# A transformer layer on one core: a third attention job in the lead, its exps held in K and V areas

## The chip, the core and the metric

The kernel runs on one core of a Trainium2 chip. The core has a matrix engine (TensorE, PE in the profile), a vector engine (VectorE, DVE), an engine for functions such as exp (ScalarE, ACT), a general one (GpSimd, POOL) and one that issues transfers (SyncE, SP). They run side by side and wait for one another by semaphores. TensorE writes its results to PSUM, eight banks of 128 x 512 fp32; everything else lies in SBUF. The metric is the device time of one execution in microseconds (us), less is better.

## What is computed

One transformer layer over 2048 tokens with 1024 features, in bf16:

```python
h  = x + softmax_attention(layernorm(x) @ wqkv) @ wo      # 32 heads of 32
h2 = h + gelu(layernorm(h) @ w1 + b1) @ w2 + b2           # 3584 hidden features
```

Softmax is over all 2048 keys, with no mask, so 32 x 2048 x 2048 exps are needed.

## The kernel before

**Units and jobs.** The tokens are cut into eight units of 256 (UNITS); heads are taken four at a time, g = 0 to 7, four heads filling the 128 partitions. A job (k, g) is the attention of unit k for head group g: eight rounds of 256 keys. One round is: `Att.qk` (L925 to L953) issues eight matmuls (QK, line L941 in the profile) into four PSUM banks, and two exps over 128 x 1024 each (L952) into a buffer PT. `Job.pv` (L989) then multiplies the exps with V (L996, PV) into a fifth bank. The softmax's denominators are sums over the keys, made by a matmul with ones (`den`, L1027, line L1036). To make it cheaper VectorE first adds the two 256-column halves of a round's exps (first-level sum, L1013), and for units below QA pairs of such sums (second-level sum, L1019); a round that is "direct" skips VectorE and goes through the ones-matmuls whole. `DIRECT` says how many of the last rounds of a job are direct (1; 3 in the very last job), `QUAD` which units have second-level sums (QA = 8: all). `finish` divides and writes the result to OT. Six PSUM banks take scores in three pairs of two; two banks (6, 7) are left for everything else, PV's result among it.

**Buffers.** There are NR = 9 PT buffers. For the lead eight more, PX 0 to 7, are laid into areas of K and V that are not written yet (L531 to L538). x tiles arrive in xrb, eight slots that overlap the later PS (VectorE's sums) and OT.

**The lead.** Before attention can run freely, x has to be normalized and projected. Sixteen tiles of 128 tokens are loaded (`x_tile`, L786), normalized on VectorE (`layer_norm`, L717: statistics L715, aggregate L724, small casts L728 to L738, a power on GpSimd L736, normalize L741), transposed on TensorE (L763) and copied from PSUM to xnT, by ScalarE (L770) for the tiles in LEAD_ACT (ten of sixteen), by VectorE (L772) for the others. For each half chunk hc (two tiles, 256 tokens) `proj_half` (L898) makes K of head group 0, and Q for hc 0 and 1; `proj_v1` (L885) makes V of group 0. As soon as a piece of K is there, the rounds of jobs (0, 0) and (1, 0) that it allows are issued: their exps go to PT and PX and are held, because the first PV waits for all projections of the lead (`pv_last`). After that come the two jobs' PVs. Before the first transposes N_WARM = 50 matmuls on zeros run (L1262).

**The rest.** ORDER (L1279) lists the jobs that run beside the projections of the further head groups (`rest_of_projections`, L1329: Q of units 0 and 1, all of K and V): (2, 0), (3, 0), then for g = 1 to 7 units 0 and 1. The weights for them are loaded after the last x tile (`rest_w`). Then unit by unit: the output projection `wo` (L1099), a second layernorm `ln2`, Q of later units (`late_q`, L844), `ffn1` and `ffn2`, beside the attention of the units that follow. K, V, xnT and the weights share their areas with the feed-forward part, so that starts only when the projections are finished. The last unit's feed-forward part has no attention beside it.

**What sets the order.** Each instruction group is a Task with an estimated duration and a priority. `Graph.schedule` (L110) runs a list scheduler over these estimates when the kernel is built, and each engine's program is emitted in the order it found; at run time an engine takes its instructions strictly in that order. VectorE, ScalarE, GpSimd and SP pick the ready task of the lowest `prio`; TensorE follows `pick_pe` (L1417): scores first, then PV by PV_BEGIN and PV_MUST, then background work by `turn`. Tables of shifts (GROUP_SHIFT, PRIO_SHIFT), keyed by the numbers of groups and tasks, move single tasks.

Of the kernel before, what the change touches and what calls it, by code (L numbers as in the profile page):

```python
# [13 lines left out]
BF = dt.bfloat16  # L14
F32 = dt.float32
# [46 lines left out]
class Graph:  # L62
# [47 lines left out]
    def schedule(self, pick_pe, pool, switch=(0.11, 0.106, 0.1), dma_rate=340.0, dma_first=1.6, dma_tail=1.0, dma_issue=0.42,  # L110
# [32 lines left out]
        while n < total:  # L143
# [5 lines left out]
            for e in self.ENGS:  # L149
                while free[e] <= now + 1e-9:  # L150
# [12 lines left out]
                    else:  # L163
                        t = min(rd, key=lambda x: (x.prio, num[x]))
                        if up and t.prio > 0:

                            for (rt, _, u) in up[:6]:
                                if u.prio < t.prio and rt < now + 0.6 * t.occ:
                                    t = None
                                    break  # L170
# [159 lines left out]
    def emit(self, e, obj):  # L330
# [10 lines left out]
PV_BEGIN = "6887668783765478677666734877585674766834855865775635885656674536"  # L341
PV_MUST = "2563656375427345237632753323452322425663763553734473555222232667"
GROUP_SHIFT = (
        "0:-229 1:131 2:136 6:-161 8:-202 9:133 11:142 14:17 15:-143 16:-115 17:-197 18:-131 20:-226 22:18 "
        "26:-18 28:-97 32:-17 33:177 34:-29 39:56 40:-11 42:55 44:53 45:81 46:22 48:243 50:-360 51:-22 "
        "55:-161 56:-142 57:-12 61:-20 66:-4 68:-18 69:18 72:-25 73:-7 76:-9 78:-61 83:-51 84:5 88:-36 "
        "89:-80 91:-37 92:-13 93:-18 94:6 95:125 98:-125 100:-193 101:-23 104:132 105:226 106:91 111:401 "
        "112:505 113:205 117:-165 118:182 120:-316 121:-313 122:-8 123:-383 124:-11 127:54 131:-14 133:-43 "
        "134:-32 135:-435 136:-33 138:-391 141:-7 145:-13 150:102 160:-184 163:3 165:232 166:-25 167:-29 "
        "169:-162 174:-10 175:592 176:-1 177:626 178:17 179:99 180:-167 182:-21 183:116 184:-46 185:11 "  # L350
        "186:24 187:-51 197:-74 198:-215 199:13 200:81 201:-20 202:4 207:-50 208:-4 209:172 211:-27 214:118 "
        "215:-55 216:-45 219:385 230:-13 231:14 232:-7 233:72 234:-5 235:78 236:-65 238:135 239:-593 240:29 "
        "241:-111 244:-185 245:112 247:-121 248:22 250:39 251:104 252:15 261:50 264:-4 268:220 270:-530 "
        "271:5 272:-920 273:1 274:-176 276:-54 277:91 279:24 281:31 293:171 294:13 295:123 296:-33 298:-6 "
        "299:111 300:113 301:2 305:321 308:34 310:17 311:10 313:52 315:-85 326:3 328:-4 329:-160 330:-11 "
# [94 lines left out]
def build_kernel(nc, A_x, A_wqkv, A_wo, B_w1, B_b1, B_w2, B_b2, out):  # L450
# [807 lines left out]
    for tt in range(4, 8):  # L1258
        x_tile(tt, -5)
# [274 lines left out]
```

## Time and profile before

| | |
|---|---|
| runs shown | 5466.11, 1078.71, 1082.22 us; median 1082.22 |
| profiled execution, its own time | 1079.89 us |
| its span | 1078.0 us |
| first exp / end of the last exp | 17.69 / 1017.7 us |
| VectorE's sums | first level x446 (439 + 7 on PX), second level x191 |
| granted TensorE clock | 1.00 |

The profile is of one execution. "Busy" is the share of the span in which an engine's instructions run; a matmul's end is modelled. A group of instructions is named by its line in the kernel, its engine and its operands (out<-in). The number after "idle before" is the time its engine stood still just before it, and the name after the arrow what ended that. The chain is the work that ended last, followed back from the end.

### The profile page before, as it was taken

The page shows a single profiled execution, that of the slowest core. Times are in us where ns is not written, and L with a number is a line of the kernel's source. Part 1 is how long each engine was busy: PE and PEld are TensorE (multiplying, and loading weights), DVE is VectorE, ACT ScalarE, POOL GpSimd, SP SyncE. Part 2 cuts the span into 40 slices and gives each one's busy share as a digit, 9 for nine tenths or more (in the row PEclk, how much of TensorE's full clock was granted, in tenths as well). Part 3 has the DMA queues.
Part 4 walks back from the last instruction along what each step waited for, and adds up shares of the span by engine and source line. Part 5 has one row for each costly group of instructions (what it writes and reads, how often), then busy time and mean ns, then how long its engine had stood idle before and what let it go on. Part 6 is the DMA issues. An engine that isn't in the chain of part 4 may idle for free.

```text
span 1078.0 us, 38343 instructions
## 1 busy us (share of the span) xinstructions
PE 1037.0 (96%) x17162; PEld 586.8 (54%) x17162; DVE 887.6 (82%) x1737; ACT 1016.2 (94%) x1121; POOL 18.8 (2%) x35
## 2 busy tenths in 40 slices
PE   7889999999999999999999999999999999999998
PEld 5546555554446645654466457456645644564483
DVE  8888677777789997998789979988997997997711
ACT  4999999999999999999999999999999999999850
POOL 2000000000000000000000000000000000000000
DMA  7910010005656575754686667558575755987640
GB/s 196 256 60 3 13 49 2 2 2 175 205 153 204 149 224 167 220 164 132 222 259 183 189 197 203 163 173 260 150 222 184 210 150 162 290 258 236 192 153 20
DMA packets 265492, 173.93 MB, mean 161 GB/s; under 512 B 26864, under 2 KB 259952, under 8 KB 264944
## 3 DMA queue, kind: packets, MB, share of 16 engines
q1 hardware_dynamic: 265328, 171.48, 53.1%
q8 instruction: 135, 2.21, 0.8%
q14 instruction: 29, 0.24, 0.1%
HBM read 161.09 MB, written 10.35 MB: 159 GB/s over the span
## 4 chain that ended last, share of the span: by engine, by line
ACT 85%; PE 10%; DVE 3%; DMA 2%; issue 0%; SPq 0%; DVEq 0%
ACT PT L952 79%; PE ps L672 5%; ACT tg L1215 4%; PE ps L669 3%; ACT PX L952 1%; PE ps L941 1%; DMA a_w1r<-in_B_w_dram 1%; DVE st L715 1%; ACT xnT L770 1%; DMA xrb<-in_A_x_dram 0%; PE ps L996 0%; DVE PS L1013 0%; DMA a_w1r<-in_A_wo_dram 0%; DVE xb L741 0%; DVE gT L1192 0%
## 5 line engine op out<-in xcount | busy, mean ns | idle before, releaser
L952 ACT ACTIVATE PT<-ps 128x1024 bf16<-128x1024 f32 x1008 | 937.4, 1148 | 5.4 <-PE ps L941 5.2
L1013 DVE TENSOR_TENSOR PS<-PT 128x1024 bf16<-128x1024 bf16 x439 | 297.4, 684 | 78.1 <-ACT PT L952 52.1
L941 PE MATMUL ps<-QT,KT 32*128 32x256 bf16 x4096 | 203.6, 273 | 13.6 <-ACT PT L952 9.9
L996 PE MATMUL ps<-PT,V 128*32 128x256 bf16 x4032 | 160.5, 273 | 2.9 <-DVE gT L1192 1.1
L941 PEld LDWEIGHTS ps<-QT,KT 32*128 32x128 bf16 x4096 | 60.8, 92 | 170.0 <-ACT PT L952 157.8
L669 PE MATMUL ps<-hnT,a_w1r 128*128 128x256 bf16 x1197 | 148.1, 273 | 1.8 <-DMA a_w1r<-in_B_w_dram 0.7
L1019 DVE TENSOR_TENSOR PS<-PS 128x1024 bf16<-128x1024 bf16 x191 | 130.8, 685 | 3.4
L669 PE MATMUL ps<-a_w2r,gT 128*128 128x512 bf16 x510 | 125.7, 380 | 3.7 <-DVE hnT L772 1.2
L669 PEld LDWEIGHTS ps<-hnT,a_w1r 128*128 128x128 bf16 x1197 | 109.2, 98 | 35.3 <-issue 20.3
L996 PEld LDWEIGHTS ps<-PT,V 128*32 128x32 bf16 x4032 | 100.9, 96 | 37.5 <-issue 6.3
L666 PE MATMUL ps<-a_w2r,gT 128*32 128x512 bf16 x1096 | 80.2, 382 | 0.4 <-DVE gT L1192 0.2
L669 PEld LDWEIGHTS ps<-a_w2r,gT 128*128 128x128 bf16 x510 | 43.8, 98 | 61.9 <-issue 15.0
L1036 PE MATMUL ps<-PS,ones 128*32 128x256 bf16 x1020 | 70.5, 274 | 0.8 <-DVE PS L1013 0.5
L1192 DVE TENSOR_TENSOR gT<-ps,b1f 128x512 bf16<-128x512 f32 x98 | 66.7, 684 | 4.8 <-PE ps L669 2.4
L666 PE MATMUL ps<-hnT,a_w1r 128*32 128x256 bf16 x1484 | 54.5, 274 | 1.7 <-DMA a_w1r<-in_B_w_dram 0.6
L1215 ACT ACTIVATE tg<-tg 128x1024 bf16<-128x1024 bf16 x49 | 55.6, 1148 | 0.0
L669 PE MATMUL ps<-xnT,Wall 128*128 128x512 bf16 (+1 forms) x241 | 51.9, 345 | 2.5 <-ACT xnT L770 1.6
L669 PE MATMUL ps<-Wall,xnT 128*128 128x256 bf16 x345 | 45.6, 274 | 1.4 <-DVE KT L819 0.8
L666 PEld LDWEIGHTS ps<-hnT,a_w1r 128*32 128x32 bf16 x1484 | 36.3, 96 | 13.4 <-issue 11.2
L666 PE MATMUL ps<-xnT,Wall 128*32 128x512 bf16 x540 | 39.1, 381 | 0.6 <-DVE KT L819 0.6
L1244 DVE SCALAR_TENSOR_TENSOR b_ost<-ps,hch 128x512 bf16<-128x512 f32 x4 | 2.8, 692 | 44.7 <-PE ps L672 44.7
L669 PEld LDWEIGHTS ps<-Wall,xnT 128*128 128x128 bf16 x345 | 31.2, 98 | 12.7 <-issue 5.1
(101 smaller groups left out, 998.0 us busy)
## 6 DMA issues: line engine op xcount, KB each, us to landing
a_w2r<-in_B_w_dram SPq DMA_DIRECT2D x105, 512.0 KB, 4.8
a_w1r<-in_B_w_dram SPq DMA_DIRECT2D x98, 512.0 KB, 4.8
a_w1r<-in_A_wo_dram SPq DMA_DIRECT2D x32, 512.0 KB, 4.5
b_w1r<-in_B_w_dram SPq DMA_DIRECT2D x14, 512.0 KB, 5.0
a_w1r<-in_A_wqkv_dram SPq DMA_DIRECT2D x11, 512.0 KB, 4.0
xrb<-in_A_x_dram SPq DMA_DIRECT2D x16, 256.0 KB, 4.1
Wall<-in_A_wqkv_dram SPq DMA_DIRECT2D x16, 256.0 KB, 4.6
hch<-in_A_x_dram SPq DMA_DIRECT2D x16, 256.0 KB, 4.4
```

Source lines behind the costliest of these rows:

```text
L666: fns.append(lambda p, j=j: p.matmul(psum[32 * j:32 * j + 32, bi(bank), c0:c1], lhsT[:, 32 * j:32 * j + 32], rhs, start=start, stop=stop, ...
L669: t.whole = lambda p: p.matmul(psum[:, bi(bank), c0:c1], lhsT, rhs, start=start, stop=stop, skip_group_check=True)
L672: t = pe(lambda p: p.matmul(psum[:, bi(bank), c0:c1], lhsT, rhs, start=start, stop=stop), occ, reads=reads, writes=[bb(bank)], mode="full" ...
L715: return dve(lambda v: v.bn_stats(st_l[:, i, 6 * c:6 * c + 6], src), 0.6, reads=[B_src], writes=[B_stl[i][c]], prio=prio)
L941: return p.matmul(psum[:, 2 * us[h // 2] + h % 2, n * i:n * i + n], KT[32 * h:32 * h + 32, g, k0:k0 + P], QT[32 * h:32 * h + 32, qs, 0:n], ...
L952: act(lambda a, u=u, k=k: a.activation(pt(s)[:, k, :, :], psum[:, 2 * u:2 * u + 2, :], ACT.Exp, bias=0.0, scale=SCALE), 1024, reads=[B_ps[ ...
L996: fns.append(lambda p, i=i, h=h: p.matmul(psum[32 * h:32 * h + 32, bi(bank), 0:nq], V[:, g, nk * r + i, 32 * h:32 * h + 32], pt(s)[:, h // ...
L1013: dve(lambda v: v.tensor_tensor(PS[:, n, :, :], pairs[:, :, 0:256], pairs[:, :, 256:512], ALU.add), c_dve(1024, 2), reads=[B_PT[2 * s], B_ ...
L1019: dve(lambda v: v.tensor_tensor(PS[:, n, :, :], PS[:, n, :, :], PS[:, m, :, :], ALU.add), c_dve(1024, 2), reads=[B_PS[n], B_PS[m]], writes ...
L1036: fns.append(lambda p, h=h, rhs=rhs, i=i: p.matmul(psum[32 * h:32 * h + 32, bi(bank), nq:2 * nq], ones32[:, :], rhs, start=False, stop=las ...
L1192: drop(dve(lambda v: v.tensor_tensor(gT[:, fc:fc + 2, cs], psum[:, bi(bank), 0:2 * n].rearrange("p (f c) -> p f c", f=2), b1f[:, fc:fc + 2 ...
L1215: act(lambda a: a.activation(t, t, ACT.Tanh, bias=0.0, scale=math.sqrt(2.0 / math.pi)), c, reads=B_t, writes=B_t, prio=-1)
```

## The change

**Lead.** Job (2, 0) joins (0, 0) and (1, 0). PX grows from eight to fourteen: K and V areas of g = 1 to 4, K of 5 to 7, V of 5, and two in slots 4 to 7 of xrb; so x tiles 12 to 15 now go to slots 0 to 3 and are loaded ahead of 8 to 11, which go to slots 4 to 7. Tile 0 is loaded in two halves, tile 1 ahead of the Q weight, tile 2 ahead of the K weight. Tiles 0 to 3 are normalized one by one in strict order. Q is made for hc 0, 1, 2 and 3 by halves (units 2 and 3 came in one projection of 512 before); for hc 0 and for all of K the matmuls are 128 columns wide. LEAD_ACT keeps tiles 0 to 3; the other twelve copies are VectorE's. ScalarE copies K and Q of hc 0 and 1 and V of the first two tiles. Warm-up matmuls: 34 instead of 50, into bank 3 instead of 4. Round 7 of job (2, 0) follows job (0, 0)'s PVs. While t < 16 us in its estimates the scheduler may hold VectorE for a more urgent task that is about to be ready.

**Sums.** The three lead jobs are direct in all rounds (no VectorE sums). Second-level sums stay for units 0 to 5 (QA = 6).

**Order of jobs.** After the lead: (3, 0); g = 1 with units 0 to 3; g = 2 to 4 with units 0 and 1; then unit 0 with g = 5 to 7, then unit 1 with g = 5 to 7. So Q of units 2 and 3 for g = 1 is made with the projections, and OT has two more slots. Mode-change costs, the transfers' sizes in the estimates and all four tables differ as well.

```diff
+LEAD_HOLD = 16.0
+LEAD_45 = 2
+LATE = 3
+DLEAD = 3
+NEX = 2
+V_ACT = 1
...
-                        if up and t.prio > 0:
+                        if up and (t.prio > 0 or e == E.DVE and now < LEAD_HOLD):
                             for (rt, _, u) in up[:6]:
-                                if u.prio < t.prio and rt < now + 0.6 * t.occ:
+                                if u.prio < t.prio and rt < now + (0.6 if t.prio > 0 else 0.4) * t.occ:
...
-    for k in range(8):
-        lo = att_lo + 2 * S * (k + 2 if k < 6 else G + k - 2)
+    px_at = [att_lo + 2 * S * a for g in range(1, 5) for a in (g, G + g)] + [att_lo + 2 * S * a for a in (5, 6, 7, G + 5)]
+    px_at += [top.cur + 2 * D * 4, top.cur + 2 * D * 6]
+    for k, lo in enumerate(px_at):
...
-    N_WARM = 50
-    LEAD_ACT = [0, 1, 2, 3, 4, 6, 8, 10, 12, 14]
+    N_WARM = 34
+    LEAD_ACT = [0, 1, 2, 3]
...
-        for dc in range(DC):
-            mm(bank, Wall[:, wp(blk), dc, 0:P], xnT[:, tc, dc, 256 * h:256 * h + 256], dc == 0, dc == DC - 1,
-               [B_W[wp(blk)][0]] + B_xnTt[tc][2 * h:2 * h + 2], True, cols=(0, 256))
+        n = P if hc == 0 or which == 1 else 256
+        for c in range(0, 256, n):
+            for dc in range(DC):
+                mm(bank, Wall[:, wp(blk), dc, 0:P], xnT[:, tc, dc, 256 * h + c:256 * h + c + n], dc == 0, dc == DC - 1,
+                   [B_W[wp(blk)][0]] + B_xnTt[tc][2 * h + c // P:2 * h + (c + n) // P], n > P, cols=(c, c + n))
...
-    QA = 8
+    QA = 6
...
-        return 0 if qb < DA else 1
+        return 16 if g == 0 and qb < DLEAD else 1
...
-    x_tile(0, -6)
+    x_tile(0, -6, 2)
+    x_tile(1, -6)
     load_w(WQ, -5, 0, P)
-    x_tile(1, -5)
+    x_tile(2, -5)
     load_w(WK, -5, 0, P)
-    x_tile(2, -5)
-    x_tile(3, -5)
-    for tt in range(4, 8):
+    for tt in range(3, 8):
         x_tile(tt, -5)
...
-        if hc == 0:
-            ln_tiles(tts[:1], -6, "dve", True)
-            ln_tiles(tts[1:], -5, "dve", True)
+        if hc < 2:
+            for tt in tts:
+                ln_tiles([tt], tt - 12, "dve", True)
...
-    ORDER = [(2, 0), (3, 0)] + [(k, g) for g in range(1, G) for k in range(2)]
+    ORDER = [(3, 0)] + [(k, g) for g in range(1, G - LATE) for k in (range(4) if g < NEX else range(2))]
+    ORDER += [(k, g) for k in range(2) for g in range(G - LATE, G)]
...
-        for k, r in {0: [(0, 0)], 1: [(0, 1), (1, 0), (1, 1)]}.get(hc, [(0, hc), (1, hc)]):
-            lead.append((k, r, att.qk((k, 0), r, NR + r if k else None)))
-    if ORDER[0] == (2, 0):
-        proj(0, 0, 1, slot(), "dve", direct=True)
-        made.append(0)
+        for k, r in {0: [(0, 0)], 1: [(0, 1), (1, 0), (1, 1)], 2: [(0, 2), (1, 2), (2, 0), (2, 1), (2, 2)]}.get(hc, [(0, hc), (1, hc), (2, hc)]):
+            if (k, r) != (2, 7):
+                lead[k, r] = att.qk((k, 0), r, None if k == 0 else NR + r if k == 1 else NR + 8 + r if r < 6 else NR - 1)
+    att.rounds = NR
+    proj_half(0, 3, slot(), "dve")
+    made.append(0)
     for hc in range(8):
-        proj_v1(2 * hc, 0, 2, slot(), "dve")
+        proj_v1(2 * hc, 0, 2, slot(), "act" if hc < V_ACT else "dve")
...
-    for k in range(2):
+    for k in range(3):
         job = Job(k, 0, slot(2))
-        for k_, r, s in lead:
-            if k_ == k:
-                job.pv(r, s)
+        for r in range(job.nr):
+            job.pv(r, lead[k, r])
+        if k == 0:
+            lead[2, 7] = att.qk((2, 0), 7)
```

## Prediction, on record before the changed kernel was seen

> **What bounds the kernel now.** I read the page first, then busy time by stage, then ScalarE's instructions in the first 30 us, then who TensorE waits for.
>
> ```profile
> span 1078.0 us, 38343 instructions
> ...
> PE 1037.0 (96%) x17162; PEld 586.8 (54%) x17162; DVE 887.6 (82%) x1737; ACT 1016.2 (94%) x1121; POOL 18.8 (2%) x35
> ...
> ACT  4999999999999999999999999999999999999850
> ...
> ACT 85%; PE 10%; DVE 3%; DMA 2%; issue 0%; SPq 0%; DVEq 0%
> ...
> L952 ACT ACTIVATE PT<-ps 128x1024 bf16<-128x1024 f32 x1008 | 937.4, 1148 | 5.4 <-PE ps L941 5.2
> ```
>
> ScalarE carries the end: 1024 exps (1008 here, 16 more into PX), full in all slices but the first and the last two. So time is won where ScalarE is not doing exps: the lead, or the tail after the last exp. The mean of 1148 ns overlaps the next instruction; a new exp starts every 0.905 us (in the fence below, four from 26.75 to the next start at 30.36), and that is its price here.
>
> ```profile
> core 0: us, PE busy (x) PEld busy (x) DVE busy (x) ACT busy (x) POOL busy (x), PEclk, DMA share, GB/s
> ...
> 51.00:61.00 10.00, 9.35 (x216) 6.57 (x217) 4.99 (x10) 9.52 (x11) 0.00 (x0) 1.00 0.68 278
> 61.00:267.00 206.00, 197.91 (x3482) 109.90 (x3473) 159.82 (x285) 205.92 (x226) 0.00 (x0) 1.00 0.10 30
> 267.00:1010.00 743.00, 723.71 (x12432) 400.12 (x12420) 663.37 (x1276) 739.18 (x805) 9.95 (x14) 1.00 0.66 197
> ```
>
> From 61 to 1010 ScalarE idles under 4 us, but TensorE only 8.1 + 19.3 = 27.4 us: a close second bound.
>
> ```profile
> 10.90 1.02 ACT L770 ACTIVATE xnT<-ps 128x1024 bf16<-128x1024 bf16 x1 [8.89 <-PE ps L763]
> ...
> 17.69 1.02 ACT L952 ACTIVATE PT<-ps 128x1024 bf16<-128x1024 f32 x1
> 18.59 1.03 ACT L770 ACTIVATE xnT<-ps 128x1024 bf16<-128x1024 bf16 x1
> 19.50 1.04 ACT L952 ACTIVATE PT<-ps 128x1024 bf16<-128x1024 f32 x1
> 22.00 1.02 ACT L770 ACTIVATE xnT<-ps 128x1024 bf16<-128x1024 bf16 x1 [1.45 <-PE ps L763]
> 24.02 1.02 ACT L952 ACTIVATE PT<-ps 128x1024 bf16<-128x1024 f32 x1 [1.00 <-PE ps L941]
> 24.94 1.02 ACT L770 ACTIVATE xnT<-ps 128x1024 bf16<-128x1024 bf16 x1
> 25.84 1.03 ACT L952 ACTIVATE PT<-ps 128x1024 bf16<-128x1024 f32 x1
> 26.75 3.80 ACT L952 ACTIVATE PX<-ps 128x1024 bf16<-128x1024 f32 x4
> 30.36 2.02 ACT L952 ACTIVATE PT<-ps 128x1024 bf16<-128x1024 f32 x2
> ```
>
> The reader sees the first exp at 17.69, copies of transposes (L770) between the exps, and waits for TensorE. By 61 us only 37 exps have started, of 48 that fit into the 43 us since the first.
>
> **The change, part by part.** The sum is made against the profiled execution: 1079.89 us, 1.89 more than its span, 2.3 under the median of 1082.22; of the other two runs shown one is 1078.71, the other no measure.
>
> *First exp earlier.* In VectorE's order tile 0's mean cast (6.92) stands behind tile 1's statistics, which wait for a transfer until 6.31, and its reciprocal (9.44) behind tile 2's; so its transposes start at 10.25. Now tile 1 is sent ahead of the Q weight and the four first tiles are normalized in strict order. From the rows: data at 3.47, two statistics 1.29, aggregate 0.21, two casts and an add near 0.4, the power on GpSimd 0.56, reciprocal and normalize 0.67, with handovers 6.8. The cover then is the warm-up: 27 of its matmuls start 0.213 us apart until 8.4, the rest 0.109 apart, so 34 of them end at 2.47 + 27 x 0.213 + 7 x 0.109 = 9.0. Tile 0's transposes start near 8.7, tile 1's follow, two copies 0.9 apart end at 11.1, K and Q in 128-column halves (second halves 16 x 0.056 = 0.9) and their copies (0.38) give the first scores at 12.5 and the first exp at 13.0: 4.7 earlier. Bounds: 1.5 (only the transposes' shift) and 5.6 (warm-up not in the way). I take 4.7, the working from rows.
>
> By the Trainium skill ("TensorE: Matmul & The Clock Gate", Part 1) matmuls run at half rate until some 3.4 us of sustained activity, and again after an idle window of that length. The trace agrees with the first half (0.213, then 0.109 after about 6 us) though its granted clock reads 1.00; if the shorter warm-up left such a gap, the lead's next 3.4 us of matmuls would take up to twice as long, by an estimate from that page 1.7 us or so off this term.
>
> *Copies.* Six copies leave ScalarE (tiles 4, 6, 8, 10, 12, 14): 6 x 0.905 = 5.4 us. Against that one V copy and one more pair of K and Q copies, 3 x 0.3 = 0.9. On VectorE the six cost 0.60 each (L772), 3.6; from its lead go 21 first-level sums and 9 second-level ones (the three lead jobs send every round's exps to the ones-matmuls directly), 30 x 0.60 = 18, most of it now after 42 us. Had VectorE no such relief, the last K half would come 3.6 later.
>
> *Third job.* Each 256-token half of K frees six exps instead of four: 6 x 0.905 = 5.4 us of ScalarE, against VectorE's feed of one half: 4 statistics 2.4, small ones 0.6, two normalizes 0.9, two copies 1.2, K and V 0.66, together 5.7. Halves 1 and 2 free 6 and 10, so ScalarE carries a stock ahead of a feed that is 0.3 slower, and the 1.45 and 1.00 waits go. I let it run through from 16.5 (second half's K; 2 exps done before). At 61 us it has started 2 + (61 - 16.5 - 0.3)/0.905 = 50.8 exps instead of 37: 13.8 x 0.905 = 12.5 us ahead, in which the first two terms are contained. Bounds: 8 (half 1 is fed as late as now, at 23.6 less the 4.7, and one hiccup per half of 0.3) and 13.5. I take 12.
>
> Cover in this stage: the held exps need buffers until the first PV, which waits for all the lead's projections. PX 0 to 11 lie in K and V of g = 1 to 4, in K of 5 to 7 and V of 5, so K of g = 1 can only be written after job 1's first PV. Today the lead's last V matmuls end near 54.9; the VectorE sums at 42.5 to 48.3 that delay the last copies are gone, so I expect about 48, lead PVs to 60, K of g = 1 from about 53. It is due when (3,0), 16 exps after the 48, is through: near 73. That wait costs nothing. SP's x tiles come in another order (12 to 15 ahead of 8 to 11), 4.1 us to landing against a half's 5.7: nothing. The weights of later g queue behind the last x tile as today.
>
> *TensorE after 61.* It must finish the same background work 12 us sooner. Removed from that stretch: QK of 6.9 rounds done earlier, each 0.218 and two mode changes of 0.13, 3.3; and the third job's PVs (8 x 0.2185) and today's sums for it (0.656), 2.4. Added: units 6 and 7 without second-level sums, 47 more groups of four ones-matmuls at 0.109, 5.1. (The lead's direct sums, 21 x 0.2185 - 12 x 0.109 = 3.3, fall before 61.) Demand 12 - 3.3 - 2.4 + 5.1 = 11.4 us out of the 27.4 idle. VectorE is relieved in units 6 and 7 by 47 x 0.60 = 28 us, which empties TensorE's two free banks sooner. No row shows how much of the idle time can be filled: between nothing (11.4 given back) and all (0). The best-filled stage has 0.8% idle, the mean is 2.9%, so up to 20 us look usable; I take a third of the demand, 4 us, as given back: nearer to all filled, since even the best stage leaves about a quarter of the mean's idle time (0.8 of 2.9) and the others start from more. Moving (2,1) and (3,1) forward and units 0 and 1 of g = 5 to 7 apart leaves 16 jobs ahead of (0,7) both ways: nothing. The tail's last second-level sum (0.6) goes, but TensorE is full there: nothing.
>
> By the Trainium skill ("Perfetto Trace Analysis", Identifying the Most-Contended Engine) headroom of TensorE is judged by weight-load share, not matmul occupancy; here that share is 53%, so nothing would be given back. TensorE's lead of the chain (10%) says otherwise.
>
> Sum: 1079.9 - 12 + 4 = 1072.
>
> **Rivals.**
> *All of it is kept* (chance 0.20). TensorE's idle time is only ScalarE's pace seen from the other side (its longest listed wait is for exps to free scores' banks, 9.9 us), and faster evictions in units 6 and 7 take 3 us off ScalarE's waits: 1079.9 - 12 - 3 = 1065. Against: 460 to 660 has under 2% idle.
> *The projections become the bound* (0.15). They end today at 267, just when job (0,7) needs the last K chunk (ScalarE waits there at 268). Demand up to that point is 12 - 5.7 + 1.7 (Q of units 2, 3 of g = 1) = 8 against 8.1 idle us. With none of it fillable, 8 to 10 go back there: 1077.
> *Slower* (0.15): TensorE is the bound from the first PV on. If that PV comes no earlier than today's 54.97, all 8.4 us of new ones-matmuls land on a full TensorE, less the 3.3 of QK: 1079.9 + 5.1 = 1085. It decides at the first PV's time. For it: 96% busy; against: 10 us of TensorE idle in the lead.
> *The lead stalls outright* on a buffer or a transfer (0.03): over 1104.
>
> **How the numbers follow.** Forecast 0.47, 1072, its own range 1068 to 1076. The range 1063 to 1083 takes in the first two rivals and the lower edge of the third, leaving out under 2 in 10. Two per cent, about what a measurement of this kernel can tell from no change, is 1060.6 to 1103.9 around the median: faster 0.03 (needs the first rival and 4 us more), slower 0.04 (the last rival and a little of the third), within 0.93.
>
> **What would show it.** First exp near 13.0 and 50 exps by 61 us (under 46: the lead term failed). Four L770 copies. First PV near 48. ScalarE's idle time in 61 to 1000 no more than 4 us above today's; if it lies before 260, the second rival is right; if late, units 6 and 7's ones-matmuls. VectorE's second-level sums 135 instead of 191, busy time down some 43 us with no effect of its own. Last exp near 1010 instead of 1017.7, the tail as long as now.

## The result and the profile after

| | before | after |
|---|---|---|
| median of 20 runs each | 1082.55 us | 1076.85 us |
| ratio | | 0.995, 95% interval 0.994 to 0.996 |
| profiled execution / its span | 1079.89 / 1078.0 us | 1075.47 / 1073.6 us |
| first exp / last exp starts | 17.69 / 1016.5 us | 15.10 / 1011.9 us |
| exps started by 61 us | 37 | 46 |

The change is 5.7 us faster in the median and 4.4 in the profiled executions. One of the 20 runs before took 5466.11 us; the ratio and its interval leave it out. Four lines of the page after it (span; busy time by engine; ScalarE's tenths in 40 slices; the chain by engine):

```profile
span 1073.6 us, 40115 instructions
...
PE 1030.0 (96%) x18065; PEld 599.5 (56%) x18131; DVE 845.1 (79%) x1668; ACT 1012.0 (94%) x1118; POOL 18.7 (2%) x36
...
ACT  5999999999999999999999999999999999999850
...
ACT 76%; PE 17%; DMA 4%; DVE 2%; issue 1%; SPq 0%; POOL 0%; POOLq 0%; DVEq 0%
```

The picture is the old one: exps from the first slice to the last but two, VectorE 42.5 us less busy. What is new is TensorE's share of the chain, 17% for 10%. Where the time was won and lost is read from the start of the n-th exp:

| exp number | 0 | 2 | 64 | 128 | 192 | 256 | 512 | 768 | 1023 |
|---|---|---|---|---|---|---|---|---|---|
| before, us | 17.7 | 24.0 | 86.0 | 144.6 | 203.5 | 262.2 | 512.3 | 763.8 | 1016.5 |
| after, us | 15.1 | 19.7 | 78.1 | 136.7 | 198.3 | 256.8 | 506.5 | 757.8 | 1011.9 |
| earlier by | 2.6 | 4.4 | 7.9 | 7.9 | 5.1 | 5.3 | 5.8 | 6.0 | 4.6 |

The lead wins 7.9 us, 2.8 go back between exps 128 and 192, 0.5 by the last exp, and the tail is as long as before. (The fall from 6.0 to 4.6 at the end is no new wait: of the tanh activations of the feed-forward part, line L1230, 15 now stand between exps 512 and 768 and 20 behind them, where 17 and 18 stood, and each takes ScalarE about 0.94 us.) The lead first: ScalarE's instructions from 9 to 20 us of the changed kernel (start, duration, engine, line, operation; in brackets the idle time before and what ended it):

```profile
9.35 1.02 ACT L767 ACTIVATE xnT<-ps 128x1024 bf16<-128x1024 bf16 x1 [7.33 <-PE ps L760]
11.55 1.02 ACT L767 ACTIVATE xnT<-ps 128x1024 bf16<-128x1024 bf16 x1 [1.18 <-PE ps L760]
13.29 0.38 ACT L920 ACTIVATE QT<-ps 128x256 bf16<-128x256 f32 x1 [0.71 <-PE ps L669]
...
14.18 1.02 ACT L767 ACTIVATE xnT<-ps 128x1024 bf16<-128x1024 bf16 x1
15.10 1.93 ACT L967 ACTIVATE PT<-ps 128x1024 bf16<-128x1024 f32 x2
16.91 1.04 ACT L767 ACTIVATE xnT<-ps 128x1024 bf16<-128x1024 bf16 x1
17.81 0.41 ACT L898 ACTIVATE V<-ps 128x256 bf16<-128x256 f32 x1
18.66 0.39 ACT L920 ACTIVATE KT<-ps 128x256 bf16<-128x256 f32 x1 [0.43 <-PE ps L669]
19.66 1.02 ACT L967 ACTIVATE PT<-ps 128x1024 bf16<-128x1024 f32 x1 [0.61 <-PE ps L956]
```

The four copies L767 are there, and the first two exps come at 15.10. The third comes only at 19.66, because tile 3's copy (16.91) stands behind those two exps and the second half's K hangs on it. TensorE in the same stretch:

```profile
8.70 0.61 PE L760 MATMUL ps<-ident,xb 128*128 128x128 bf16 x8
9.15 0.60 PE L1276 MATMUL ps<-b2t,ident 128*128 128x256 bf16 x4
10.52 0.55 PE L669 MATMUL ps<-xnT,Wall 128*128 128x128 bf16 x7 [0.77 <-ACT xnT L767]
10.90 0.61 PE L760 MATMUL ps<-ident,xb 128*128 128x128 bf16 x8
```

Tile 1's transposes (10.90) stand behind seven matmuls of tile 0's projection, which wait for tile 0's copy. Then the stages:

```profile
12.00:61.00 49.00, 40.92 (x708) 29.25 (x708) 36.52 (x103) 45.86 (x54) 4.48 (x7) 1.00 0.83 223
...
61.00:267.00 206.00, 200.92 (x3816) 117.18 (x3824) 154.58 (x281) 203.64 (x223) 0.00 (x0) 1.00 0.11 34
267.00:1010.00 743.00, 719.05 (x12996) 407.18 (x13032) 632.73 (x1222) 738.60 (x804) 9.13 (x14) 1.00 0.66 196
```

The columns are, after the stretch and its length, busy PE, PEld, DVE, ACT and POOL, then clock, DMA share and GB/s. From 61 to 267 us ScalarE now idles 2.36 us, where it idled 0.08. The whole of it is four waits for scores:

```profile
141.18 44.10 ACT L967 ACTIVATE PT<-ps 128x1024 bf16<-128x1024 f32 x48 [0.50 <-PE ps L956]
185.85 3.77 ACT L967 ACTIVATE PT<-ps 128x1024 bf16<-128x1024 f32 x4 [0.57 <-PE ps L956]
190.31 5.60 ACT L967 ACTIVATE PT<-ps 128x1024 bf16<-128x1024 f32 x6 [0.69 <-PE ps L956]
196.51 71.61 ACT L967 ACTIVATE PT<-ps 128x1024 bf16<-128x1024 f32 x78 [0.60 <-PE ps L956]
```

In the program these are four rounds whose two exps stand in swapped order on ScalarE. The next QK writes banks that the exp now second still reads, so it has to wait for both exps and ScalarE waits for the QK.

### The profile page after: what moved, and what is told of

Its sections match the earlier page's. It is cut to its first block, busy times and chain, and to the rows that moved or that the text cites. A ratio compares the mean times of both kernels' runs of the same rounds, so it can differ in the third digit from the quotient of the medians.

```text
span 1073.6 us, 40115 instructions
## 1 busy us (share of the span) xinstructions
PE 1030.0 (96%) x18065; PEld 599.5 (56%) x18131; DVE 845.1 (79%) x1668; ACT 1012.0 (94%) x1118; POOL 18.7 (2%) x36
## 4 chain that ended last, share of the span: by engine, by line
ACT 76%; PE 17%; DMA 4%; DVE 2%; issue 1%; SPq 0%; POOL 0%; POOLq 0%; DVEq 0%
ACT PT L967 71%; PE ps L666 5%; PE ps L669 5%; ACT tg L1230 3%; PE ps L663 2%; PE ps L956 2%; DMA a_w1r<-in_B_w_dram 2%; PE ps L1011 1%; ACT PX L967 1%; PE ps L1276 1%; DMA a_w1r<-in_A_wo_dram 1%; PE ps L1051 1%; DMA Wall<-in_A_wqkv_dram 0%; DMA a_w2r<-in_B_w_dram 0%; DMA q_scratch<-a_ost 0%
## 5 line engine op out<-in xcount | busy, mean ns | idle before, releaser
L967 ACT ACTIVATE PT<-ps 128x1024 bf16<-128x1024 f32 x996 | 925.4, 1150 | 8.6 <-PE ps L956 8.5
L666 PE MATMUL ps<-hnT,a_w1r 128*128 128x256 bf16 x1086 | 132.7, 273 | 2.4 <-DMA a_w1r<-in_B_w_dram 1.3
L666 PEld LDWEIGHTS ps<-hnT,a_w1r 128*128 128x128 bf16 x1086 | 99.6, 98 | 30.8 <-issue 15.2
L666 PE MATMUL ps<-a_w2r,gT 128*128 128x512 bf16 x434 | 108.2, 380 | 7.3 <-issue 3.3
L1034 DVE TENSOR_TENSOR PS<-PS 128x1024 bf16<-128x1024 bf16 x135 | 92.5, 685 | 2.5
L666 PEld LDWEIGHTS ps<-a_w2r,gT 128*128 128x128 bf16 x470 | 40.3, 98 | 56.0 <-issue 12.6
L663 PE MATMUL ps<-hnT,a_w1r 128*32 128x256 bf16 x1928 | 68.6, 274 | 2.2 <-DVE gT L1207 1.0
L663 PEld LDWEIGHTS ps<-hnT,a_w1r 128*32 128x32 bf16 x1928 | 47.3, 96 | 15.2 <-issue 13.2
L1230 ACT ACTIVATE tg<-tg 128x1024 bf16<-128x1024 bf16 x49 | 55.4, 1162 | 0.0
L1259 DVE SCALAR_TENSOR_TENSOR a_ost<-ps,hch 128x512 bf16<-128x512 f32 x28 | 19.2, 686 | 38.8 <-PE ps L666 30.6
L666 PE MATMUL ps<-xnT,Wall 128*128 128x512 bf16 (+1 forms) x182 | 43.1, 366 | 3.3 <-issue 1.3
L663 PEld LDWEIGHTS ps<-a_w2r,gT 128*32 128x32 bf16 x1256 | 27.5, 96 | 23.2 <-issue 13.9
L666 PE MATMUL ps<-a_w1r,OT 128*128 128x512 bf16 x161 | 39.7, 381 | 0.4 <-DVE OD L1083 0.3
L1051 PEld LDWEIGHTS ps<-PS,ones 128*32 128x32 bf16 x1160 | 30.6, 96 | 14.8 <-issue 3.4
```

The source lines that it names most:

```text
L663: fns.append(lambda p, j=j: p.matmul(psum[32 * j:32 * j + 32, bi(bank), c0:c1], lhsT[:, 32 * j:32 * j + 32], rhs, start=start, stop=stop, ...
L666: t.whole = lambda p: p.matmul(psum[:, bi(bank), c0:c1], lhsT, rhs, start=start, stop=stop, skip_group_check=True)
L967: act(lambda a, u=u, k=k: a.activation(pt(s)[:, k, :, :], psum[:, 2 * u:2 * u + 2, :], ACT.Exp, bias=0.0, scale=SCALE), 1024, reads=[B_ps[ ...
L1034: dve(lambda v: v.tensor_tensor(PS[:, n, :, :], PS[:, n, :, :], PS[:, m, :, :], ALU.add), c_dve(1024, 2), reads=[B_PS[n], B_PS[m]], writes ...
L1051: fns.append(lambda p, h=h, rhs=rhs, i=i: p.matmul(psum[32 * h:32 * h + 32, bi(bank), nq:2 * nq], ones32[:, :], rhs, start=False, stop=las ...
L1230: act(lambda a: a.activation(t, t, ACT.Tanh, bias=0.0, scale=math.sqrt(2.0 / math.pi)), c, reads=B_t, writes=B_t, prio=-1)
```

## The experiments

Two theories stood at the start: A, a microsecond won in the lead arrives at the end, less what the stretch 140 to 200 us takes; and B, TensorE's projections are the bound until 267 us and take any lead back. Medians in us, beside the median of the kernel before in the same comparison; exp times from the profile, the changed kernel's on top:

| run | median | before | ratio (95%) | exp 0 | exp 2 | exp 64 | exp 192 | by 61 us |
|---|---|---|---|---|---|---|---|---|
| changed kernel | 1076.85 | 1082.55 | 0.995 (0.994 to 0.996) | 15.1 | 19.7 | 78.1 | 198.3 | 46 |
| e1_t1first | 1076.45 | 1082.53 | 0.9948 (0.9933 to 0.9964) | 14.5 | 19.1 | 78.4 | 198.7 | 46 |
| e2_la10 | 1082.12 | 1082.53 | 1.0009 (0.9993 to 1.0024) | 13.9 | 18.4 | 83.5 | 203.9 | 40 |
| e3_vhalf | 1125.17 | 1082.53 | 1.0395 (1.0371 to 1.0419) | 14.3 | 18.9 | 77.6 | 198.0 | 46 |
| e4_control | 1119.97 | 1082.53 | 1.0353 (1.0333 to 1.0373) | 14.9 | 19.5 | 78.4 | 198.7 | 46 |
| f1_lead2 | 1076.14 | 1081.67 | 0.9959 (0.9945 to 0.9973) | 15.1 | 18.5 | 78.3 | 198.6 | 46 |
| f2_unswap | 1075.69 | 1081.67 | 0.9952 (0.9938 to 0.9966) | 13.5 | 18.0 | 77.6 | 197.7 | 46 |
| f3_both | 1076.42 | 1081.67 | 0.9958 (0.9943 to 0.9974) | 15.1 | 18.1 | 77.8 | 197.9 | 46 |
| f4_ones32 | 1075.87 | 1081.67 | 0.9955 (0.9939 to 0.9972) | 14.4 | 19.0 | 78.0 | 198.3 | 46 |
| g1_stats | 1075.08 | 1081.34 | 0.9942 (0.9928 to 0.9957) | 14.6 | 19.2 | 77.1 | 197.3 | 47 |
| g2_stats_both | 1074.23 | 1081.34 | 0.9941 (0.9923 to 0.9959) | 13.6 | 16.9 | 76.4 | 196.3 | 48 |
| g3_loads | 1076.08 | 1081.34 | 0.995 (0.9934 to 0.9967) | 15.0 | 18.0 | 77.5 | 197.6 | 46 |
| h1_pvnarrow | 1077.24 | 1081.13 | 0.9953 (0.9934 to 0.9973) | 14.1 | 18.6 | 77.2 | 197.6 | 47 |

**Tile 1 first.**

```diff
-            proj_half(0, 0, 0, ev)
+            proj_half(0, 0, 0, ev, t1_last)
```

(the first matmul of this piece waits for the last task on TensorE before it, tile 1's transposes)

> The changed kernel with one order added: tile 1's transposes ahead of tile 0's Q projection on TensorE (there they start at 10.90 us although their data is there near 8.95, behind a projection that waits for ScalarE's copy). Both theories: the first exp comes about 1.1 us earlier, near 14.0. Theory A (a us won in the lead arrives at the end, less what the projections of 140 to 200 us take back): 0.4 to 1.1 us faster than the changed kernel. Theory B (the projections are the bound, so whatever the lead wins is lost there): no change at the end, and ScalarE's idle time in 61 to 267 us grows by about 1.

The edit did not bring about what it was for: the scheduler now put the other of tile 0's two pieces there, and tile 1's transposes still stood behind seven matmuls. 46 exps by 61 us, 1076.45 us: near to a repeat of the changed kernel.

**Ten copies on ScalarE again.**

```diff
-    LEAD_ACT = [0, 1, 2, 3]
+    LEAD_ACT = [0, 1, 2, 3, 4, 6, 8, 10, 12, 14]
```

> The changed kernel with six copies of transposes put back on ScalarE (LEAD_ACT as before). Both: about 5.4 us (6 x 0.905) fewer exps started by 61 us, 40 instead of 46. Theory A: the copies cost 5.4 at the end, near 1080 to 1082. Theory B: TensorE's projections hold ScalarE up less when it comes later, so the 2.8 us lost in 128 to 192 exps come back and the end is only 2 to 3 us later, near 1079.

Exp 64 is 5.4 us later than in the changed kernel, the price of six copies at 0.905, and 40 exps start by 61 us; that it fits to the digit is luck, since this run began its exps 1.2 us earlier. The same four waits are there, 2.5 us in all, though everything comes 5.5 us later: so they are not a price of being early, which speaks against theory B. At the end the two theories are not told apart. In the median nothing is left of the gain (ratio 1.0009), as theory A asked; but eleven of this run's twelve executions have a mean granted clock of 0.997 or 0.998, and the profiled one, at 1.00, is 3.2 us slower than the changed kernel's (1078.67 for 1075.47), its last exp 3.2 us later. So 2.4 of the 5.6 us by which exp 192 was late came back behind exp 256, and the order of this run, which the scheduler found anew, can have a part in both.

**Less projection work, and a control.** The first leaves out half of the sum over features in V of groups 4 and 5; the second leaves out nothing and only changes two estimates of the scheduler in the third digit.

```diff
-                mm(bank, xnT[...], Wall[...], dc == 0, dc == DC - 1,
+                m = mm(bank, xnT[...], Wall[...], dc == 0, dc == nd - 1,
...
-    gr.schedule(pick_pe, pool_banks, (0.111337, 0.111675, 0.1))
+    gr.schedule(pick_pe, pool_banks, (0.114476, 0.110146, 0.1))
```

> The changed kernel that leaves out half of the sum over features in V of head groups 4 and 5: 64 matmuls of 256 columns, 6.9 us of TensorE, in the projections. If TensorE's work is the bound there (theory B), the 2.8 us that ScalarE loses between its 128th and 192nd exp come back: 2 to 4 us faster than the changed kernel, and what is left out is more than is needed. If the loss is one of order or of evictions by VectorE, not of work: under 1 us.

> The changed kernel with the scheduler's two mode-change costs of the kernel before (0.1145 and 0.1101 in place of 0.1113 and 0.1117): no work is changed, only the order that comes out of the estimates. It shows what a changed order alone is worth, for the reading of the other variants, whose orders were not tuned either. Expected 0 to 4 us slower than the changed kernel; if it is more, differences of a few us between variants say nothing of the part that was changed.

Both are 43 to 48 us slower than the changed kernel, so the first says nothing on its question: a new order came with the missing work. The control is the finding. Its exp 64 (78.4) and exp 192 (198.7) are the changed kernel's, but from 400 us on it falls behind, 21 us at exp 768 and 26 at the last; the rest comes in the tail, 83 us from the last exp to the end for 62. In its profile the granted clock stood at 0.50 in 20.5 us of this time, so a part of the loss may be the clock's. ScalarE's longest waits in the control (total, times, longest):

```profile
ACT gT L1213 <- PE ps L666: 23.7, 2, 18.5
ACT PT L967 <- PE ps L956: 19.6, 30, 1.3
ACT PT L967 <- PE ps L1011: 10.6, 2, 7.5
```

In the changed kernel the second of these is 8.5 us in 15 waits. The tables of shifts did not carry over to the order that this change of the estimates gave. So every kernel from here on kept the emitted order except at the places named: tasks were moved or narrowed after the order had been found.

**The lead's order.** Tile 1's transposes ahead of tile 0's projection, tile 3's behind the first QK, tile 3's copy ahead of the first exps:

```diff
+    move(pe_q, t1, gr.tasks[90])
+    move(pe_q, t3, pe_q[pe_q.index(first) + 1])
+    move(act_q, [gr.tasks[160]], next(t_ for t_ in act_q if t_.kind == "exp"))
```

> The changed kernel with three places of its order edited and nothing else moved, re-estimated or left out: on TensorE the eight transposes of tile 1 stand ahead of the projection piece of tile 0, the eight of tile 3 stand right behind the first QK, and on ScalarE tile 3's copy stands ahead of the first two exps. In the changed kernel the third exp starts at 19.66 us, 1.8 later than two exps behind the first would let it. Theory A (a microsecond won in the lead arrives at the end of the program, because ScalarE is the bound of all that follows): third exp at 17.6 to 18.2 us, exps 64 and 128 earlier by 1.3 to 1.8 us, and the median 1.0 to 1.8 us under the changed kernel's 1076.85 us, 1075.0 to 1075.9. Rival (TensorE's backlog of projections takes every lead won back before 267 us): the exps around index 256 no earlier than in the changed kernel, more ScalarE idle time between 61 and 267 us than its 2.36, and a median of 1076.5 to 1077.2.

The third exp came at 18.55, 1.1 us earlier, and stayed ahead until exp 20. By exps 22 and 24 it was all lost again (39.00 us and 41.74, where the changed kernel has 38.81 and 41.57). TensorE just before that:

```profile
35.81 1.89 PE L669 MATMUL ps<-xnT,Wall 128*128 128x128 bf16 x16
37.49 1.06 PE L669 MATMUL ps<-Wall,xnT 128*128 128x128 bf16 x8
```

The same matmuls take 1.07 us (from 36.70) and 0.61 (from 37.61) in the changed kernel. Here TensorE ran at half its rate from 35.25 to 38.66 us, where the granted clock is 0.50 (last section). So this profile tests neither theory: the lead was lost ahead of the projections of 61 to 267 us, but at least in part to the clock of this one execution. The median is 5.5 us under the kernel before, no better than the changed kernel's 5.7.

**The swapped rounds.** The two exps change places in eleven rounds, and the next QK moves ahead of 0.55 to 0.87 us of matmuls:

```diff
+            act_q[i_], act_q[i_ + 1] = b_, a_
...
+            pe_q.remove(t_)
+            pe_q.insert(j_, t_)
```

> The changed kernel with its order edited at eleven rounds: in each the two exps of one round stand in swapped order on ScalarE, and the next QK, which writes the banks of one of them, has to wait for both. Here the two exps change places and the next QK moves ahead of some 0.55 to 0.87 us of other matmuls; nothing is left out. In the changed kernel four of these rounds lie between 137 and 193 us, and ScalarE's only four waits between 61 and 267 us, 2.36 us in all, lie right behind them. Theory S (the swapped rounds took 2.4 of the 2.8 us that are given back between exps 128 and 192): the four waits are gone, under 0.5 us of ScalarE idle time is left between 61 and 267 us, exp 192 is 2.0 to 2.6 us earlier, the median is 1074.0 to 1075.2 us. Rival (TensorE is short of time there, and the swaps only show where it falls due): 1.5 us or more of waits come back at other rounds before 267 us, and the median stays at 1076.3 to 1077.5.

> The edits of the lead's order and of the eleven swapped rounds together; nothing is left out. If theory A and theory S both hold, the gains add up: exp 256 earlier by 3.3 to 4.4 us than in the changed kernel, median 1072.5 to 1074.0 us, under both kernels. If TensorE's backlog is the bound until 267 us, at most one of the two gains is seen at exp 256 and the median is 1075 to 1077 us.

The four waits shrank from 2.36 to 1.8 us (ScalarE's whole idle time from 61 to 267 us is 1.97), and exps 128 to 192 took 61.5 us for 61.7: a miss for theory S, with as much waiting left as the rival asked for. TensorE around the first of the four places shows why:

```profile
139.47 0.40 PE L956 MATMUL ps<-QT,KT 32*128 32x256 bf16 x8
139.80 0.29 PE L1051 MATMUL ps<-PS,ones 128*32 128x256 bf16 x4
139.92 0.83 PE L1011 MATMUL ps<-PT,V 128*32 128x256 bf16 x24
140.68 1.38 PE L666 MATMUL ps<-Wall,xnT 128*128 128x256 bf16 x11
141.99 0.40 PE L956 MATMUL ps<-QT,KT 32*128 32x256 bf16 x8
```

The QK that was moved is early now (139.47), but what it jumped over still lies ahead of the one after it: 2.52 us from QK to QK, where two exps take 1.81. The wait moved on by one round. TensorE is busy all the time between these two QKs, so in this order the amount of its work may count; no run took work away from it here. The lead's edits and the swaps together began the third exp at 18.1 and, at full clock, were 1.3 us ahead at exp 22; at exp 64 only 0.2 us was left. TensorE of the run with the swapped rounds undone, and then VectorE of the run with both, at 40 us:

```profile
39.06 0.29 PE L669 MATMUL ps<-Wall,xnT 128*128 128x128 bf16 x2
40.17 1.02 PE L666 MATMUL ps<-xnT,Wall 128*128 128x512 bf16 x4 [0.82 <-DVE tb L726]
```

```profile
37.69 0.69 DVE L712 BATCH_NORM_STATS2 st<-xrb 128x6 f32<-128x512 bf16 x1
39.45 0.42 DVE L901 CAST V<-ps 128x256 bf16<-128x256 f32 x1 [1.07 <-PE ps L669]
```

A projection of 512 columns (L666) waits, in the program, for VectorE's copy of the V piece just before it (L901) and for the fifth of the late weight loads. In the changed kernel the weight ended that wait, 0.98 us at 40.59; here TensorE waits for the copy while VectorE waits for the end of TensorE's V piece, a round trip. With VectorE relieved (below), 0.52 of its 0.82 us stay.

**Cheaper ones-matmuls.** Those of units 6 and 7 that read first-level sums take 32 columns for 256, which leaves out most of these denominators:

```diff
+            w = 32 if self.qb > 5 and not direct else nq
```

> The changed kernel in its own order, in which the ones-matmuls of units 6 and 7 that read first-level sums take 32 columns in place of 256, so most of the denominators of these two units are left out. It takes away about as much TensorE time as the change added by giving up the second-level sums of two units (my estimate 4 to 5 us, all of it behind 700 us). Theory A (ScalarE is the bound there and TensorE's added work costs nothing): the median within 0.8 us of the changed kernel's, 1076.0 to 1077.6. Rival (the added ones-matmuls are a part of what was given back): 2 to 4.5 us faster, 1072.5 to 1075.

TensorE's busy time from 700 to 1010 us fell from 303.2 to 298.9 us, and the median is 5.80 us under the kernel before, as the changed kernel's is 5.70. So the rival's 2 to 4.5 us are not there, and in the median the 5.1 us of matmuls that came with giving up two units' second-level sums cost nothing that can be seen within an interval of some 1.8 us either way. The profile leaves room for a part. Up to exp 832 the two kernels run alike (821.84 and 821.95 us), but the last exp starts 1.35 us earlier (1010.54 for 1011.89), and from exp 896 to the last ScalarE waits 0.06 us, for 1.03 in the changed kernel and 1.8 in two other runs of the same order (short statistics, narrow PVs). With one profile of each that stays open.

**Cheaper statistics, and earlier weights.** Three tests of what holds the lead at 40 us. The first two read 128 of each 512 columns, in the changed kernel's order and in that of both edits together; the third moves SyncE's first store of xnT behind five weight loads.

```diff
-                half_stats(i + k, c, x_ap[:, 512 * c:512 * c + 512], B_x[c], prio)
+                half_stats(i + k, c, x_ap[:, 512 * c:512 * c + (128 if B_o in B_xb else 512)], B_x[c], prio)
...
+    sp_q.remove(store)
+    sp_q.insert(sp_q.index(gr.tasks[773]) + 1, store)
```

> The changed kernel in its own order, but the row statistics of the first norm read 128 of each 512 columns, so three quarters of x are left out of the means and variances; nothing else changes. VectorE stands at 100% busy from 22 to 38 us in the changed kernel, without a wait, and 30 statistics instructions of 670 ns lie there; between the rows of 147 ns for two columns and 670 ns for 512, 128 columns should take about 280 ns, 11 us of VectorE less in the lead. Theory V (since the copies moved, VectorE's work in the lead is what holds ScalarE back there): ScalarE's waits of 1.9 us between 19.6 and 61 us go down to under 0.6, exp 64 is 1.3 us or more earlier than 78.1, and 47 or 48 exps start by 61 us. Rival D (the weights' landing, or TensorE's own work, holds it): the waits around 40 us stay at 1 us or more and exp 64 moves by less than 0.7 us. If what is won by exp 64 reaches the end, the median is 1074.5 to 1075.7 us, if not, 1076.2 to 1077.

> The order of the run with the lead's and the swapped rounds' edits together, and the short statistics as well (three quarters of x left out of the means and variances of the first norm). There the third exp started at 18.12 us, 1.5 earlier than in the changed kernel, but TensorE waited for VectorE at 40 us and exp 64 was only 0.3 earlier. Theory V: with VectorE relieved the lead's gain is kept, exp 64 is 2.0 to 3.5 us earlier than in the changed kernel, 48 or 49 exps start by 61 us. Rival D: exp 64 is less than 1 us earlier. If the gain reaches the end, the median is 1073.3 to 1074.8 us; if projections take it back, 1075.5 to 1077 us.

> The order of the run with the lead's and the swapped rounds' edits together, nothing left out, and on SyncE's queue the first 1 MB store of the transposed x stands behind five weight loads and not ahead of them; the store waits for VectorE's copy, and the DMA engines stood at a share of 0.23 from 22 to 26 us while those loads stood behind it. Rival D (the weights' landing holds the lead): the wait of TensorE at 40 us is gone and exp 64 is 0.8 to 1.5 us earlier than in the same order without this edit (77.8). Theory V (VectorE holds it): weights land 3 to 5 us earlier, TensorE waits for VectorE as before, exp 64 within 0.4 us of 77.8. The median is 1075.0 to 1076.0 us under D and 1075.8 to 1077 us under V.

VectorE in the changed kernel, and in the run with the short statistics and both edits (stretch, length, busy time and instructions, clock, DMA share, GB/s):

```profile
30.00:34.00 4.00, 4.00 (x15) 1.00 0.96 320
34.00:38.00 4.00, 4.00 (x13) 1.00 1.14 257
38.00:42.00 4.00, 3.98 (x15) 1.00 0.91 205
```

```profile
30.00:34.00 4.00, 3.16 (x12) 1.00 1.10 244
34.00:38.00 4.00, 2.13 (x9) 1.00 0.91 204
38.00:42.00 4.00, 3.90 (x15) 1.00 1.05 237
```

A statistics instruction took 271 ns instead of 670. With that, exp 64 came 1.0 us earlier than in the changed kernel (between the two theories' numbers) and 1.7 with both edits (under the 2.0 expected). How much of that is VectorE's has to be read beside the first exp, which differs from run to run whatever the edit (last section). The first of the two doesn't settle it: the run with narrow PVs, whose lead is untouched, has exp 64 at 77.2 as well. The second began at 13.6 and has exp 64 at 76.4; the run with only the swapped rounds undone began at 13.5 and has it at 77.6. Against the run with both edits and whole statistics exp 64 moved from 77.8 to 76.4, but its first exp was 1.5 us earlier too. So VectorE's load holds 1.5 us of the lead at most, part of this can be the early start, and one profile each is little to go by. The round trip stays: with VectorE relieved TensorE still waits 0.52 us for the V copy, at 38.55. Earlier weights alone gave 0.4 at exp 64 (rival D had asked for 0.8, theory V for 0.4 at most), TensorE still waited 0.61 us for the copy, and the fifth load landed only 1.1 us earlier (38.24 us for 39.34; I had expected 3 to 5). The gain of the second run lived to exp 832 (2.3 us) and was 1.2 at the last exp; its ratio (0.9923 to 0.9959) can't be told from the changed kernel's. No run beats the changed kernel by more than its interval.

**Narrow PVs.** PV matmuls planned between 61 and 200 us take 32 columns for 256, which leaves out seven eighths of these products:

```diff
+            def w():
+                return 32 if 61 < me[0].done < 200 else nq
...
-                        psum[32 * h:32 * h + 32, bi(bank), 0:nq], V[:, g, nk * r + i, 32 * h:32 * h + 32],
+                        psum[32 * h:32 * h + 32, bi(bank), 0:w()], V[:, g, nk * r + i, 32 * h:32 * h + 32],
```

> The changed kernel in its own order, in which the PV matmuls that are planned between 61 and 200 us take 32 columns in place of 256, so seven eighths of those products are left out; nothing else changes. By the run with narrow ones-matmuls (4.3 us less TensorE busy time for 448 matmuls of the same width) some 76 rounds of eight should give TensorE about 5.9 us back in that stretch. Theory T (what is given back between exps 128 and 192 is TensorE's own work, more between two QKs at four places than ScalarE's two exps cover): the four waits of 2.36 us go under 1.0, exp 192 is 1.3 to 2.5 us earlier than 198.3, and if a gain before 200 us reaches the end the median is 1074.4 to 1075.6. Rival W (a wait that does not hang on the amount of work, such as a late weight or a late copy, sets those four places): the waits stay at 2 us or more and exp 192 moves by less than 0.5 us, median 1076.2 to 1077.2.

TensorE's busy time from 61 to 200 us fell by 10.1 us (5.9 expected), from 135.5 to 125.4. ScalarE's waits there:

```profile
140.44 44.10 ACT L967 ACTIVATE PT<-ps 128x1024 bf16<-128x1024 f32 x48 [0.51 <-PE ps L956]
185.12 3.77 ACT L967 ACTIVATE PT<-ps 128x1024 bf16<-128x1024 f32 x4 [0.57 <-PE ps L956]
189.57 5.61 ACT L967 ACTIVATE PT<-ps 128x1024 bf16<-128x1024 f32 x6 [0.69 <-PE ps L956]
195.78 71.61 ACT L967 ACTIVATE PT<-ps 128x1024 bf16<-128x1024 f32 x78 [0.59 <-PE ps L956]
```

The same four, to 0.01 us (its exps are 0.7 us earlier in this stretch, after a first exp at 14.08). Rival W is right about the waits: in this order they do not hang on how much TensorE has to do, but on exp, QK, exp following one another at a swapped round. The median, 1077.24 us, gained nothing.

## Why the prediction was right, and where it failed

Within 2% was right (chance 0.93), and 1076.85 lies in the range of 1063 to 1083, just outside the likeliest case's own, 1068 to 1076. The sum was 1079.9 - 12 + 4 = 1072 against the profiled execution; it measured 1079.9 - 7.9 + 3.3 = 1075.3, near its own 1075.47. The interval of the ratio, 0.994 to 0.996, also tells a change of half a per cent from none, which is far less than the two per cent that I had set as the limit. That forecast and result lie this close is partly luck: the lead gave 4 us less than was put down for it, and the 3.3 us that went back did so for a reason that the working did not have.

*First exp: 13.0 expected, 15.10 measured, 13.5 to 15.1 over the profiled runs.* Tile 0's transposes started at 8.70, as worked out. From there I gave 4.3 us to the first exp; it took 6.40. The step that failed is "tile 1's follow, two copies 0.9 apart end at 11.1": tile 1's transposes stood behind seven matmuls that wait for tile 0's copy, and the second copy ended at 12.57, 1.5 of the 2.1 us too late. Most of the rest lies behind it, where tile 2's copy (14.18) stands ahead of the first exp on ScalarE. I worked along the data and not along TensorE's queue.

*Copies: right at exp 64.* 5.4 us, shown by their return to ScalarE; of that, 3.2 us is seen at the end of the profiled executions.

*Third job: the lead term failed in size, 7.9 us for 12, at the edge of its bounds.* "I let it run through from 16.5" was the step: the third exp came at 19.66, 3.2 us late, and 1.5 us of waits and a copy followed by 61 us, so that 46 exps had started and not 50.8. My test, under 46, was just not met. The lower bound had the right size by accident, since it supposed a late half 1 and not a queue's order. That the order was not all shows in two runs at full clock that pulled the third exp forward by 1.5 and 1.6 us: 1.0 to 1.3 us of it was lost by exp 64, most of that around 40 us, to the round trip of a V copy, with VectorE's load and the weights falling due at the same time; their shares stay open. How much the third job adds by itself is not shown: the earlier first exp (2.6 us) and the copies (5.4) already make up the 7.9, and no run leaves that job out.

*First PV: 48 expected, 56.24 measured.* A clear miss; before it was 54.97. By my own condition (no earlier than today's) the slower rival, 1085, should have come true. It did not, because its price was wrong: most of the 5.1 us of ones-matmuls in units 6 and 7 left out moved the median by 0.1 us and the last exp by 1.35. (The 3.3 us of them in the lead were not tested.) Why the first PV was late shows in the trace: between 47 and 56 us VectorE, whose sums I had taken for the delay, waits for TensorE six times, 0.89 to 1.05 us each, while QKs ahead of the last projections wait for ScalarE's exps (0.71 us at 48.14, 0.69 at 51.81). That points to TensorE's queue again.

*TensorE after 61: the size was nearly right, 3.3 us for 4, the cause was not.* I priced the work TensorE must do. 10.1 us less of it in the stretch changed none of the waits, and 4.3 us less of it late moved the last exp by 1.35 us and the median not at all. 2.36 of the 2.8 us lie at four rounds whose order makes ScalarE, TensorE and ScalarE wait in turn; the kernel before has no such wait from 61 to 267 us. The idle time does lie before 260, as the second rival asked, but that rival's cause, a shortage of TensorE time, is refuted by the run with narrow PVs for the order as it stands. That a better order takes these 2.4 us back was not shown: undoing the swaps moved three quarters of the wait to the next QK, behind 2.5 us of TensorE's work, and there a shortage is not ruled out: swaps undone and narrow PVs were not run together.

I set the Trainium skill ("Perfetto Trace Analysis", Identifying the Most-Contended Engine) aside because TensorE had 10% of the chain. That was the wrong reading: a share of a chain counts dependencies as well as work. With weight loads at 56% of the span the run with narrow PVs agrees with its rule, there was headroom at the four waits; the time went back all the same, so headroom by that measure did not mean that nothing is given back.

*The rest:* four copies, 135 second-level sums, VectorE 42.5 us less busy (43 expected) and the tail's length were right, and so was the bound on ScalarE's idle time: by the stages' rows it is 6.8 us from 61 to 1010 us for 3.9, 2.9 more (4 at most expected). The last exp ended at 1013.0, 3 us later than the forecast of 1010 in place of 1017.7.

## What to carry to other kernels

Where each engine takes its instructions in a fixed order, work out a moved step along each engine's queue, not along its data: what stands ahead of it there, and what that waits for. Before a wait is put down to an engine's load, take work from that engine without touching the order; if the wait stays to the hundredth of a microsecond, it is not the load. Compare the granted clock of the two stretches first: one of these profiles lost its lead at half clock. And when a schedule has been tuned by tables, compare variants only in the same emitted order, since a third digit of an estimate cost 43 us here.

## What the hardware showed unexpectedly

In nine of the profiles the order up to the first exp is the changed kernel's. In these it came between 13.53 and 15.10 us, and 6.3 to 6.4 us behind the start of tile 0's transposes. The spread lies in the warm-up matmuls, the first 30 of which took 6.34 us in the changed kernel and 4.77 in the run with the swapped rounds undone, where the first exp started at 13.53:

```profile
2.53 6.34 PE L1276 MATMUL ps<-b2t,ident 128*128 128x256 bf16 x30 [2.53 <-POOL b2t L699]
8.70 0.61 PE L760 MATMUL ps<-ident,xb 128*128 128x128 bf16 x8
```

```profile
2.52 4.77 PE L1276 MATMUL ps<-b2t,ident 128*128 128x256 bf16 x30 [2.52 <-POOL b2t L699]
7.13 0.61 PE L760 MATMUL ps<-ident,xb 128*128 128x128 bf16 x8
```

They start 0.213 us apart at first and 0.109 apart later; the step came at 8.47 us in one and at 5.27 in the other, after 28 and 13 matmuls. The profile's granted clock reads 1.00 all through, since the traces hold no record of the slow stretch; in the changed kernel's trace the first record, of 1.00, starts at 8.48. The Trainium skill ("TensorE: Matmul & The Clock Gate", Part 1: The HAM clock gate) says that the number of slow matmuls varies from run to run with the phase of a free-running window; the traces agree, with 13 to 28 slow ones over the thirteen profiles after the change. The slow stretch lasted 5.94 us in the one and 2.75 in the other, where the prediction had taken some 3.4 us from that page; the measurement decides. The moment of the step moved the first exp by up to 1.6 us, but not all of it lasts: three runs with the same lead began their exps at 14.08, 14.40 and 15.10 and had exp 64 at 77.2, 78.0 and 78.1.

The half-rate stretch after a shorter warm-up that I had weighed did not come in the changed kernel: tile 1's transposes ran at 0.056 us each. But one came later in the profile of the run with the lead's order edited (stretch, length, busy PE, PEld, DVE, ACT and POOL, clock, DMA share, GB/s):

```profile
31.84:35.25 3.41, 1.71 (x33) 1.11 (x25) 3.41 (x13) 3.41 (x5) 1.16 (x2) 1.00 1.12 248
35.25:38.66 3.41, 3.40 (x36) 2.75 (x40) 2.65 (x9) 2.71 (x3) 0.00 (x0) 0.50 0.89 200
```

The clock's records in this trace start at 7.95, 35.25 and 38.66 us, eight steps and one step of 3.41 us apart. TensorE was not idle in the 3.41 us before the fall: it was busy for half of them. Such stretches bear on the comparison too. Of the 62 executions of the kernel before that were run beside the variants, 30 have a mean clock under 1.00, and their median is 1083.0 us, for 1080.4 of the others; of the changed kernel's 20 it is 2. With a clock of 1.00 the medians lie 4.1 us apart (1080.4 and 1076.4), near the 4.4 of the two profiled executions. So a part of the 5.7 us may be that the changed kernel falls to half clock less often; no run was made to test that.
